# Low halves of stored second-layer weight operands: a subtraction on VectorE or GpSimd, or a negated copy and an accumulating transfer

## The chip, the cores and the metric

The kernel runs on one NeuronCore of a Trainium2 chip. The metric is the device time of one execution in microseconds; the profile comes from one execution taken by the hardware profiler. TensorE multiplies matrices (PE is its matmul row, PEld its weight loads), VectorE is DVE, ScalarE is ACT, GpSimd is POOL, and SyncE, SP, issues transfers here.

## The reference

Attention with two kinds of mask feeds a mixture of four experts without a choice among them: every expert is computed for every token and weighted.

```python
def _attn_ref(q, k, v):                      # (4, 8, 576, 64) float32
    scores = scale * np.matmul(q, k.transpose(0, 1, 3, 2))
    ...                                      # heads 0-3: the last 32 keys; heads 4-7: every 32nd key
    attn = softmax(np.where(masks, scores, -1e9))
    return np.matmul(attn, v)

def _moe_ref(x, domain_probs, w1, w2):       # x (2304, 512), w1 (4, 512, 1024), w2 (4, 1024, 512)
    p = domain_probs / (domain_probs.sum(-1, keepdims=True) + 1e-09)
    for e in range(E):
        h = np.maximum(x @ w1[e], 0.0)
        out += p[:, e:e + 1] * (h @ w2[e])
```

## The kernel before

Every large product is made in three matmul passes: each operand is split into a high half (the value rounded to the type fp32r) and a low half (the value minus its high half), and high x high, low x high and high x low are added in PSUM. An expert's 1024 hidden columns are two units of 512, so there are eight units, 0 to 7.

The tokens are worked in three parts. In the first part, to about 194 us, attention runs and the first 384 tokens go through all units as plain products. The middle part works 896 tokens, unit after unit in the order 7, 0, 1, ..., 6 (the list `first_order`). Its first layer is a Strassen-like scheme of seven products on quarters of the weights and of the inputs (`plan_unit`, products by `product`, line 1082); its second layer is plain (`plan_mm2`, `mm2_t`, line 929). The last part, from about 475 us, works 1024 tokens with the seven-product scheme in both layers and reads its weight operands back from DRAM: `d1` holds the operands of the first layer, `d2` those of the second. The middle part makes them and stores them.

`plan_keep2` is called once for each unit of the middle part. It stores three quarters of the second-layer weights as they are (from the tile `w2t`, whose halves the middle part computes anyway, line 883). The four other operands, s1 to s4, are sums and differences of quarters of `raw2`. Each is built in one of three buffers `tmp` (tokens ws0, ws1, ws2; ws0 is used for s1 and for s4; lines 823 and 826). The function `split` writes its high half by a copy on ACT (line 818) and its low half by a subtraction on DVE or POOL (line 819) into one of the two buffers `wv`, and SP stores that buffer to `d2` (line 894). Operands 0 and 2 use `wv` buffer 0, operands 1 and 3 buffer 1. The same `tmp` buffers are used by `plan_w1` for the first-layer operands of the next unit (tiles s1 to s4, called s in the trace).

In a unit of the middle part the seven products come first (16.8 us) and then the second layer (19 us). ACT copies finished product sums from PSUM into the buffers `u` (line 1284), so that the next product can add into the same bank; it also rounds weights and applies the relu (line 917). DVE joins sums (line 1297), makes low halves of activations (line 920) and accumulates outputs (line 938).

No engine's order is written by hand. The class `Plan` takes operations by `add(engine, duration, function, tokens read, tokens written, priority, ...)` and simulates them at build time with the durations given: at each step the engine and operation that can start first are taken, ties go by priority. An operation of engine "VP" goes to DVE or POOL, whichever would finish it first. An operation with `xfer` is a transfer: to the duration of its issue come 0.7 us, the time given, and 1.4 us until its end. PE's matmuls of the mixture are one fixed list. The result is the order in which each engine's instructions are emitted; at run time each engine works its list in order and waits on semaphores. The dictionary `SHIFT` adds amounts to the priority of single operations, by the operation's number in the order of the `add` calls. Its last entries, 814 to 842, belong to the weights of unit 0, whose operations follow the first call of `plan_keep2` in the numbering.

Of the kernel before, what the change touches and what calls it, by code (L numbers as in the profile page):

```python
# [8 lines left out]
F32 = mybir.dt.float32  # L9
F32R = mybir.dt.float32r  # L10
BF16 = mybir.dt.bfloat16
AF = mybir.ActivationFunctionType
ALU = mybir.AluOpType
# [30 lines left out]
class Plan:  # L44
# [24 lines left out]
    def add(self, eng, dur, fn, reads=(), writes=(), prio=0.0, bank=None, moe=False, cols=0, xfer=None, two=False, lead=None, lag=0.0):  # L69

        o = Op()
        o.eng, o.dur, o.fn, o.prio, o.moe = eng, dur, fn, prio, moe
        o.bank = () if bank is None else bank if isinstance(bank, list) else [bank]
        o.start = None
        o.cols = cols  # L80
        o.xfer = xfer
        o.two = two or eng == "VP"
        o.ready = 0.0
        o.nxt = []
        o.idx = len(self.ops)
        o.prio += SHIFT.get(o.idx, 0.0)
        pre = set()
        for r in reads:
            if r in self.writer:
                pre.add(self.writer[r])  # L90
        for w in writes:
            if w in self.writer:
                pre.add(self.writer[w])
            pre.update(self.readers.get(w, ()))
        pre.discard(o)
        for r in reads:
            self.readers.setdefault(r, []).append(o)
        for w in writes:
            self.writer[w] = o
            self.readers[w] = []  # L100
        o.kind, o.lead, o.early, o.lag = eng, lead, 0.0, lag
        o.wait = o.pre = len(pre)
        for p in pre:
            p.nxt.append(o)
        self.ops.append(o)
# [222 lines left out]
def attn_moe_kernel(  # L328
# [14 lines left out]
    nc = tc.nc  # L343
# [8 lines left out]
    scale = 1.0 / float(D) ** 0.5  # L352
# [77 lines left out]
    add = plan.add  # L430

    def engine(e):
        return nc.vector if e == "DVE" else nc.gpsimd
# [381 lines left out]
    def split(src, tok, hi, lo, name, z):  # L815

        need = [tok, "late1"] if name in ("s1", "s2", "s4") or name[:2] == "wv" else [tok]
        add("ACT", 0.62, lambda: nc.scalar.activation(out=hi(), in_=src(), func=AF.Copy), need, [name + "h"], z)  # L818
        add("VP", VP, lambda e: engine(e).tensor_tensor(  # L819
            out=lo(), in0=src(), in1=hi().bitcast(F32), op=ALU.subtract), need + [name + "h"], [name + "l"], z)  # L820

    def combine(dst, a, b, toks, tok, z):
        add("VP", VP, lambda e: engine(e).tensor_tensor(out=dst(), in0=a(), in1=b(), op=ALU.subtract), toks, [tok], z)

    def total(dst, a, b, toks, tok, z):
        add("VP", VP, lambda e: engine(e).tensor_tensor(out=dst(), in0=a(), in1=b(), op=ALU.add), toks, [tok], z)  # L826
# [24 lines left out]
    def plan_w1(z, step, plain):  # L851

        def t(i):
            return lambda: tmp["s", i]

        if plain:
            plan_quarter(A11, "raw10", "a11", z)
        total(t(0), A21, A22, ["raw10", "raw11"], "ws0", z + step)
        plan_quarter(t(0), "ws0", "s1", z + step)
        combine(t(1), t(0), A11, ["raw10", "ws0"], "ws1", z + 2 * step)  # L860
        plan_quarter(t(1), "ws1", "s2", z + 2 * step)
        if plain:
            plan_quarter(A12, "raw11", "a12", z + 3 * step)
        combine(t(2), A11, A21, ["raw10"], "ws2", z + 4 * step)
        plan_quarter(t(2), "ws2", "s3", z + 4 * step)
        if plain:
            plan_quarter(A22, "raw11", "a22", z + 5 * step)
        combine(t(0), A12, t(1), ["raw11", "ws1"], "ws0", z + 6 * step)
        plan_quarter(t(0), "ws0", "s4", z + 6 * step)
# [9 lines left out]
    def plan_keep2(u, z, step):  # L879


        for n, (nm, i, j) in enumerate((("a11", 0, 0), ("a12", 0, 1), ("a22", 1, 1))):
            add("SP", 0.4, lambda nm=nm, i=i, j=j: nc.sync.dma_start(
                out=d2[u, nm].rearrange("p j h c -> p (j h) c"),
                in_=w2t[:, 2 * j:2 * j + 2, :, 256 * i:256 * i + 256].rearrange("p j h c -> p (j h) c").bitcast(F32)),
                [f"w2{2 * j + a}{h}" for a in range(2) for h in "hl"], [f"d2{u}{nm}"], z + 2 + n, xfer=((1.6, 512),))

        def t(i):
            return lambda: tmp["s", i]

        def keep(n, nm):
            v = n % 2
            split(t((0, 1, 2, 0)[n]), f"ws{(0, 1, 2, 0)[n]}", lambda: late["wv"][v][:, :, 0], lambda: late["wv"][v][:, :, 1], f"wv{v}", z + n * step)
            add("SP", 0.4, lambda: nc.sync.dma_start(out=d2[u, nm], in_=late["wv"][v].bitcast(F32)), [f"wv{v}h", f"wv{v}l"], [f"d2{u}{nm}"],
                z + n * step + 2, xfer=((1.45, 128),))

        total(t(0), B21, B22, ["raw20", "raw21", "late2"], "ws0", z)
        keep(0, "s1")
        combine(t(1), t(0), B11, ["raw20", "raw21", "ws0"], "ws1", z + step)
        keep(1, "s2")  # L900
        combine(t(2), B11, B21, ["raw20", "raw21"], "ws2", z + 2 * step)
        keep(2, "s3")
        combine(t(0), B12, t(1), ["raw20", "raw21", "ws1"], "ws0", z + 3 * step)
        keep(3, "s4")
# [90 lines left out]
    late = {}  # L995
# [369 lines left out]
    for u in range(NU):  # L1365
        z = Z0 + ZU * u
# [6 lines left out]
    z = Z0 + ZU * NU  # L1373
# [128 lines left out]
```

## Time and profile before

| | us |
|---|---|
| Median of 3 runs | 791.96 |
| Lowest and highest run | 791.91, 792.69 |
| Span of the profiled execution | 790.3 |
| Median of the runs over that span | 1.66 |
| PE busy in the span | 780.0 |
| DVE, ACT, POOL busy in the span | 604.0, 325.0, 353.5 |

The span runs from the first to the last instruction of the profiled execution. Busy time of one engine overlaps that of the others. Matmuls are pipelined and their ends are modelled, so a busy PE is not PE at its peak.

### The profile page before, as it was taken

The numbers are of one execution on the slowest core, as the hardware profiler recorded it, in microseconds if no ns is written. First come the engines' busy times: TensorE is split into PE (matmuls) and PEld (weight loads), VectorE is DVE, ScalarE is ACT, GpSimd is POOL, SyncE is SP. The second block draws the span as 40 slices with busy tenths as digits, with TensorE's granted clock in tenths as the row PEclk, the third lists the DMA queues.
The fourth block names the chain that finished last, engine by engine and source line by source line (L and its number), as shares of the span: only waits on it lengthen the run. The fifth ranks groups of instructions, "written<-read, shape, count | busy, mean of one in ns | idle before, by whom it ended". The sixth has DMA issues, their size and how long they took to land.

```text
span 790.3 us, 13805 instructions
## 1 busy us (share of the span) xinstructions
PE 780.0 (99%) x5374; PEld 663.7 (84%) x5377; DVE 604.0 (76%) x828; ACT 325.0 (41%) x597; POOL 353.5 (45%) x265
## 2 busy tenths in 40 slices
PE   7999999999999999999999999999999999999998
PEld 5788888899888889898988888888888888888886
DVE  6988867796888586867768593958787869687886
ACT  4645454653534445263535452524141423232330
POOL 6334223682755152534425170708180817172672
PEclk9999999999999999999999999999999999999999
DMA  9777553157779687775963415837374647555525
GB/s 336 276 272 255 198 180 123 61 199 266 287 276 341 205 302 246 286 262 218 316 217 102 164 40 185 289 140 265 138 268 157 236 162 238 190 183 197 176 80 186
DMA packets 70720, 168.32 MB, mean 213 GB/s; under 512 B 5216, under 2 KB 24320, under 8 KB 70656
## 3 DMA queue, kind: packets, MB, share of 16 engines
q1 hardware_dynamic: 70512, 167.34, 60.4%
q8 instruction: 42, 0.69, 0.3%
q14 instruction: 22, 0.18, 0.1%
q10 hardware_dynamic: 144, 0.11, 0.1%
HBM read 107.64 MB, written 59.79 MB: 212 GB/s over the span
## 4 chain that ended last, share of the span: by engine, by line
PE 97%; DVE 1%; ACT 0%; issue 0%; POOL 0%; DVEq 0%; ACTq 0%
PE mo L1082 23%; PE mo L929 18%; PE ps L1082 18%; PE sc L1082 15%; PE mo L913 9%; PE ps L929 5%; PE sc L929 5%; PE ps L705 2%; PE ps L673 1%; PE sc L561 1%; PE sc L550 1%; PE mo L1408 0%; PE ps L640 0%; DVE wv L819 0%; DVE mx L578 0%
## 5 line engine op out<-in xcount | busy, mean ns | idle before, releaser
L1147 POOL TENSOR_TENSOR q<-q,q 128x512 f32<-128x512 f32 x41 | 60.9, 1492 | 142.4 <-DVE q L1116 141.5
L929 PE MATMUL mo<-w2t,h 128*128 128x512 f32 x336 | 80.8, 389 | 0.0
L929 PEld LDWEIGHTS mo<-w2t,h 128*128 128x128 f32 x336 | 63.1, 188 | 13.0
L929 PE MATMUL mo<-w2t,hs 128*128 128x512 f32 x288 | 70.9, 397 | 0.0
L920 DVE SCALAR_TENSOR_TENSOR h<-c,h 128x448 fp32r<-128x448 f32 x48 | 61.6, 1311 | 2.4 <-ACT h L917 1.0
L929 PEld LDWEIGHTS mo<-w2t,hs 128*128 128x128 f32 x288 | 52.8, 188 | 11.3
L819 POOL TENSOR_TENSOR w2t<-raw,w2t 128x512 fp32r<-128x512 f32 x21 | 31.4, 1503 | 61.4 <-ACT w2t L818 51.3
L819 POOL TENSOR_TENSOR a<-raw,a 128x512 fp32r<-128x512 f32 x17 | 27.7, 1629 | 57.1 <-DVE c L1297 55.4
L1113 DVE TENSOR_TENSOR q<-ps,v 128x512 f32<-128x512 f32 x48 | 33.1, 690 | 25.3 <-PE ps L1082 24.8
L938 DVE SCALAR_TENSOR_TENSOR acc<-mo,pr,acc 128x512 f32<-128x512 f32 x45 | 33.6, 746 | 24.3 <-PE mo L929 24.0
L818 ACT ACTIVATE w2t<-raw 128x512 fp32r<-128x512 f32 x60 | 37.4, 632 | 33.0 <-PE mo L929 18.6
L1208 DVE TENSOR_TENSOR acc<-sc,acc 128x512 f32<-128x512 f32 x57 | 38.5, 685 | 15.7 <-PE sc L1082 15.5
L1104 ACT ACTIVATE v<-mo 128x512 f32<-128x512 f32 x48 | 28.5, 594 | 48.2 <-PE mo L1082 48.2
L913 PE MATMUL mo<-xh,a 128*128 128x384 f32 x192 | 45.5, 340 | 0.0
L1116 DVE SCALAR_TENSOR_TENSOR q<-q,pb 128x512 f32<-128x512 f32 x48 | 42.4, 884 | 1.6
L818 ACT ACTIVATE wv<-tmp 128x512 fp32r<-128x512 f32 x32 | 20.1, 631 | 52.9 <-POOL tmp L826 8.0
L929 PE MATMUL ps<-w2t,h 128*128 128x512 f32 x168 | 40.4, 389 | 0.0
L929 PE MATMUL sc<-w2t,h 128*128 128x512 f32 x168 | 40.4, 389 | 0.0
L1142 ACT ACTIVATE Tb11h<-q 128x512 fp32r<-128x512 f32 x16 | 10.0, 628 | 70.6 <-DVE q L1116 70.6
L1147 DVE TENSOR_TENSOR q<-q,q 128x512 f32<-128x512 f32 x23 | 32.7, 1421 | 6.7 <-POOL Tb21l L1143 6.4
L929 PEld LDWEIGHTS ps<-w2t,h 128*128 128x128 f32 x168 | 31.5, 188 | 6.5
L929 PEld LDWEIGHTS sc<-w2t,h 128*128 128x128 f32 x168 | 31.5, 188 | 6.5
(281 smaller groups left out, 2052.9 us busy)
## 6 DMA issues: line engine op xcount, KB each, us to landing
raw<-in_w SPq DMA_DIRECT2D x28, 1024.0 KB, 6.5
qkS<-in_qk_strided SPq DMA_DIRECT2D x16, 329.0 KB, 7.3
out<-acc SPq DMA_DIRECT2D x17, 256.0 KB, 2.0
vstL<-in_v_local SPq DMA_DIRECT2D x6, 640.0 KB, 5.7
vstS<-in_v_strided SPq DMA_DIRECT2D x8, 384.0 KB, 5.6
qkL<-in_qk_local SPq DMA_DIRECT2D x7, 416.0 KB, 6.2
pb<-dp SPq DMA_DIRECT2D x5, 512.0 KB, 7.6
qkL<-in_qk_local SPq DMA_DIRECT2D x10, 208.0 KB, 5.5
```

The source lines that it names most:

```text
L818: add("ACT", 0.62, lambda: nc.scalar.activation(out=hi(), in_=src(), func=AF.Copy), need, [name + "h"], z)
L819: add("VP", VP, lambda e: engine(e).tensor_tensor(out=lo(), in0=src(), in1=hi().bitcast(F32), op=ALU.subtract), need + [name + "h"], [name ...
L913: nc.tensor.matmul(pt[:, 0:TA], w[:, c % 2, (f % 2) * P:(f % 2) * P + P], (xl if i == 1 else xh)[c], start=j == 0, stop=j == 11)
L920: nc.vector.scalar_tensor_tensor(out=dst(), in0=src(), scalar=0.0, in1=hi().bitcast(F32), op0=ALU.max, op1=ALU.subtract)
L929: nc.tensor.matmul(pt, ht[f][:, ts], wt[f][:, cs], start=j == 0, stop=j == 11)
L938: nc.vector.scalar_tensor_tensor(out=a, in0=pt, scalar=sc, in1=a, op0=ALU.mult, op1=ALU.add)
L1082: nc.tensor.matmul(pt, a[i == 2][:, j, f * P:f * P + P], skewed(b[i == 1][j], TH)[:, cs], start=bool(first) and n == 0, stop=True, skip_gr ...
L1104: add("ACT", TH2 / 1200 + 0.18, lambda: nc.scalar.activation(out=late["u"][i], in_=held[key][:, 0:TH2], func=AF.Copy), [key, "late3"], [f" ...
L1113: add("DVE", DD, lambda: nc.vector.tensor_tensor(out=q(), in0=src(), in1=late["u"][i], op=ALU.add), [key, f"u{i}", "late3"], [tok], min(zz ...
L1116: add("DVE", DD, lambda: nc.vector.scalar_tensor_tensor(out=q(), in0=q() if from_q else src(), scalar=0.0, in1=late["p"][:, c * TH2:c * TH ...
L1147: add("VP", VP, lambda e: engine(e).tensor_tensor(out=dst[0](), in0=a[0](), in1=b[0](), op=ALU.subtract), [a[1], b[1]], [dst[1]], zz - 2.4)
L1208: add("DVE", DD, lambda i=i, key=key: nc.vector.tensor_tensor(out=acc[i], in0=held[key][:, 0:TH2], in1=acc[i], op=ALU.add), [key], tok, zd)
```

## The change

The four operands s1 to s4 of each unit no longer go through `split` but through a new function, `split_moved`. ACT writes the negated, rounded operand into the place of the low half, then the high half as before. A transfer issued from GpSimd's queue then adds the operand itself (fp32, in `tmp`) to the negated high half in place, from SBUF to SBUF: the result is the operand minus its high half, as before. The planner is given 1.0 us on POOL for the issue and 1.5 us for the transfer. It sees one operation more for each operand, so four more for each unit.

```diff
+    def split_moved(src, tok, hi, lo, name, z):
+
+        add("ACT", 0.62, lambda: nc.scalar.activation(out=lo(), in_=src(), func=AF.Copy, scale=-1.0), [tok, "late1"], [name + "l"], z)
+        add("ACT", 0.62, lambda: nc.scalar.activation(out=hi(), in_=src(), func=AF.Copy), [tok, "late1"], [name + "h"], z)
+        add("POOL", 1.0, lambda: nc.gpsimd.dma_start(out=lo().bitcast(F32), in_=src(), accum_op=ALU.add), [tok, name + "l"], [name + "l"], z,
+            xfer=((1.5, 128),))
+
...
         def keep(n, nm):
             v = n % 2
-            split(t((0, 1, 2, 0)[n]), f"ws{(0, 1, 2, 0)[n]}", lambda: late["wv"][v][:, :, 0], lambda: late["wv"][v][:, :, 1], f"wv{v}", z + n * step)
+            split_moved(t((0, 1, 2, 0)[n]), f"ws{(0, 1, 2, 0)[n]}", lambda: late["wv"][v][:, :, 0], lambda: late["wv"][v][:, :, 1], f"wv{v}", z + n * step)
             add("SP", 0.4, lambda: nc.sync.dma_start(out=d2[u, nm], in_=late["wv"][v].bitcast(F32)), [f"wv{v}h", f"wv{v}l"], [f"d2{u}{nm}"],
                 z + n * step + 2, xfer=((1.45, 128),))
```

## Rows read from the trace of the kernel before

**Rows 1.** The page: span, busy times, chain that ended last.

```profile
span 790.3 us, 13805 instructions
...
PE 780.0 (99%) x5374; PEld 663.7 (84%) x5377; DVE 604.0 (76%) x828; ACT 325.0 (41%) x597; POOL 353.5 (45%) x265
...
PE 97%; DVE 1%; ACT 0%; issue 0%; POOL 0%; DVEq 0%; ACTq 0%
```

**Rows 2.** Waits of PE from 190 us to the end: total us, times, longest.

```profile
PE mo L1082 <- ACT u L1284: 0.4, 1, 0.4
```

**Rows 3.** Busy time by stretches: stretch, its length, engines, PE clock, DMA share, GB/s.

```profile
390.00:410.00 20.00, 20.00 (x91) 16.64 (x90) 15.32 (x21) 6.26 (x11) 9.50 (x8) 1.00 0.64 238
...
195.00:446.00 251.00, 250.64 (x1174) 219.81 (x1174) 190.19 (x239) 115.46 (x207) 112.00 (x77) 1.00 0.70 248
```

**Rows 4.** Groups of instructions, 195 to 446 us: the operands' copies and subtractions.

```profile
L818 ACT ACTIVATE wv<-tmp 128x512 fp32r<-128x512 f32 x32 | 20.1, 631 | 52.9 <-POOL tmp L826 8.0 <-POOL tmp L823 6.8 <-DMA d25s<-wv 6.0
...
L819 DVE TENSOR_TENSOR wv<-tmp,wv 128x512 fp32r<-128x512 f32 x24 | 25.6, 1068 | 1.8 <-ACT wv L818 1.8
...
L819 POOL TENSOR_TENSOR wv<-tmp,wv 128x512 fp32r<-128x512 f32 x8 | 11.3, 1412 | 51.2 <-ACT wv L818 51.2
```

**Rows 5.** The tile wv: durations min/median/max ns, and its stores' landing.

```profile
L819 DVE TENSOR_TENSOR wv<-tmp,wv x24: 681/1120/1757, 196.3 to 438.3; 128x512 fp32r<-128x512 f32 x24
L819 POOL TENSOR_TENSOR wv<-tmp,wv x8: 1288/1293/1752, 202.9 to 404.3; 128x512 fp32r<-128x512 f32 x8
...
L894 SPq DMA_DIRECT2D d25s<-wv x4: 320/320/320, 396.9 to 405.6; - x4
...
DMA to landing us min/median/max: 2.6/3.1/5.3
```

**Rows 6.** Transfers by issue: KB each, median us to landing.

```profile
out<-acc SPq DMA_DIRECT2D x17, 256.0 KB, 2.0
```

**Rows 7.** ACT in order of time, 390 to 426 us: start, us, line.

```profile
394.75 0.63 ACT L818 ACTIVATE wv<-tmp 128x512 fp32r<-128x512 f32 x1 [1.34 <-POOL tmp L826]
...
402.36 0.63 ACT L818 ACTIVATE wv<-tmp 128x512 fp32r<-128x512 f32 x1 [5.34 <-DMA d25s<-wv]
...
407.87 2.67 ACT L818 ACTIVATE w2t<-raw 128x512 fp32r<-128x512 f32 x4 [3.64 <-PE ps L929]
411.12 0.55 ACT L1284 ACTIVATE u<-mo 128x448 f32<-128x448 f32 x1 [0.57 <-PE mo L1082]
...
414.32 0.63 ACT L818 ACTIVATE s<-tmp 128x512 fp32r<-128x512 f32 x1 [0.93 <-PE sc L1082]
415.92 0.55 ACT L1284 ACTIVATE u<-mo 128x448 f32<-128x448 f32 x1 [0.97 <-PE mo L1082]
```

**Rows 8.** POOL in order of time, 390 to 426 us.

```profile
394.79 1.56 POOL L823 TENSOR_TENSOR tmp<-tmp,raw 128x512 f32<-128x512 f32 x1
397.05 1.28 POOL L823 TENSOR_TENSOR tmp<-raw,tmp 128x512 f32<-128x512 f32 x1 [0.70 <-DVE wv L819]
```

**Rows 9.** PE in order of time, 408 to 426 us.

```profile
414.52 0.56 PE L1082 MATMUL mo<-t2h,s 128*128 128x448 f32 x2
...
419.32 0.56 PE L1082 MATMUL mo<-t3h,s 128*128 128x448 f32 x2
```

**Rows 10.** The first two units: ACT and PE in order of time.

```profile
195.68 0.62 ACT L818 ACTIVATE wv<-tmp 128x512 fp32r<-128x512 f32 x1
...
205.79 0.52 ACT L1284 ACTIVATE u<-mo 128x448 f32<-128x448 f32 x1
...
206.21 0.54 ACT L1284 ACTIVATE u<-ps 128x448 f32<-128x448 f32 x1
206.36 0.68 PE L1082 MATMUL mo<-t4h,a 128*128 128x448 f32 x2 [0.36 <-ACT u L1284]
...
220.72 0.63 ACT L818 ACTIVATE wv<-tmp 128x512 fp32r<-128x512 f32 x1 [3.41 <-DVE tmp L826]
...
231.75 0.55 ACT L1284 ACTIVATE u<-ps 128x448 f32<-128x448 f32 x1
```

## The prediction

> **What bounds the kernel now.** I read the page first. The span is 790.3 us, the matmul row is busy for 780.0 us of it, and the chain that ended last is 97% PE [rows 1]: before and after the middle part the reader should look for one thing only, what makes PE late. The median of the runs, 791.96 us, lies 1.66 us above the span of the profiled execution. I make the sum on the span and add those 1.66 us.
>
> The waits of PE from 190 us on hold a single entry, 0.4 us on ACT [rows 2]. The table by stretches says the same: from 195 to 446 us, the middle part with its eight units, PE is busy 250.64 of 251.00 us at granted clock 1.00, the 2.4 GHz level, while DVE has 190 us of work, ACT 115 and POOL 112, and the DMA engines are 70% busy [rows 3]. The order of PE's work is a fixed list and none of its matmuls changes. So at most 0.36 us can be won, and the question is whether the longer way of the low halves makes PE wait.
>
> **What is removed.** 32 subtractions (four in each of eight units): 24 on DVE, 1068 ns each, 25.6 us, and 8 on POOL, 1412 ns, 11.3 us [rows 4]. Neither engine was the bound, so they are worth nothing directly; a DVE with 25 us more air is worth nothing either, as PE waited on DVE nowhere [rows 2].
>
> **What is added on ACT.** A second copy for each operand, of the shape of the hi copy, which takes 631 ns [rows 4]: 32 x 0.631 = 20.2 us, and ACT goes from 115 to 136 us in 251 us. The trace shows no copy with a scale; I take it as this row, between the 0.55 us of a 448-column copy and the 0.67 us of a w2t copy [rows 7]. From the second unit on these copies lie in the stretch of second-layer matmuls, where ACT is busy for only 6.26 of 20 us [rows 3]; that idle time hides them. In the first unit nothing does (below).
>
> **What is added on POOL.** 32 transfers, each a 256 KB read, added to 256 KB in place. No transfer of this queue and no accumulating one stands in the trace. How long POOL is held by the issue: from below SP's issue, 0.32 us, from above the longest POOL subtraction, 1.75 us [rows 5]; I take 1.3, an ordinary POOL operation. From the issue's end to the landing: from below 2.0 us, a 256 KB transfer of SP's queue [rows 6], from above 5.3 us, the slowest 512 KB store of the same tile [rows 5]; I take its median, 3.1, since an accumulating 256 KB touches more bytes than a plain one. Call issue to landing T: 2.3 to 7.05, taken as 4.4 us. POOL gets 32 x 1.3 = 42 us and loses 11.3: 143 of 251 us, still idle for four tenths. Behind the waiting transfer stand POOL's own sums and low halves. It waits for ACT's negated copy, 0.63 us, and the flexible operations can go to DVE, which has just lost 25 us. I charge nothing; without that cover it would be at most 0.63 us per transfer on weights that PE needs a phase later. On the DMA engines 8.4 MB are read, added and written in 251 us, at 248 GB/s and 0.70 before [rows 3]; counted as two plain copies that is at most 0.19 more, about 0.89, inside the spread of T.
>
> **What moves: the chain of one unit.** I follow the unit at 390 us (operands of unit 5). Before, the store is issued 2.2 us after the copy starts [rows 5, 7]; now a whole T comes between. The negated copy starts at 394.75 [rows 7], and POOL is in a sum until 396.35 [rows 8]. Issue there, landing at 396.35 + T, store landing 3.1 us later [rows 5]. The second operand's negated copy can start at 396.35, its transfer behind the first about 397.7, its store lands at 400.8 + T. Only then does buffer 1 take the fourth operand: its transfer is issued at about 401.5 + T and lands at 401.5 + 2T, and only then is the first sum buffer free for the next unit's weights.
>
> Who waits for that, in ACT's order: four w2t copies (2.67 us from 407.87), the copies of PSUM into u at 411.12 and 415.92, and the first s copy, at 414.32 [rows 7]. PE writes again into those PSUM banks at 414.52 and 419.32 [rows 9]. The w2t copies may slide until 414.52 - 0.55 - 2.67 = 411.3; the fourth operand's two copies end at 402.1 + T, so T up to 9.2 is hidden. The s copy may slide until 419.32 - 0.55 - 0.63 = 418.1, its sum before it (0.68 us at the shortest on DVE for this shape [rows 5]) must start at 417.4: 401.5 + 2T = 417.4 gives **T = 7.9**. At 4.4 the first sum buffer is free at 410.3, four us before the s copy's old place. So this unit and those like it lose nothing at the value that I take, nor at the top of my bounds, 7.05. Past 7.9 every microsecond of T costs up to two per unit, in the five units 1 to 5; unit 6 has no next unit.
>
> Two units are tighter. In unit 0 the first copy stands 11.03 us ahead of the first u copy (220.72, 231.75), against 16.37 in unit 5 (394.75, 411.12) [rows 7, 10]: 5.3 us less, so its limit is 7.9 - 2.7 = 5.2. Price 0 at 4.4, 3.7 at 7.05; I take 0.3. The first unit works its operands among the products. Its copy starts at 195.68 [rows 10]; with T = 4.4 the first transfer, issued at 196.3, lands at 200.7, the store at 203.8, and the third and fourth operands' four copies (2.5 us) fall between 203.9 and 206.9. There the u copies at 205.79 and 206.21 have no slack: PE waits 0.36 us for them already [rows 10]. Price from -0.36 (that wait disappears) to 3.9 (two copies, 1.26, and a wait of 7.05 - 4.4); I take 0.6.
>
> **The hand-made shifts.** The table SHIFT goes by an operation's number. The first unit gets four more operations, so its eight entries from 814 to 842, which lay on the second unit's weights, now lie on operations four places earlier in the list: a store of the first unit and other splits of the same weights. These weights are made most of a unit ahead of their use. Price 0; to both sides 0.4, the one wait that there is [rows 2].
>
> **The queues passed.** SP's stores of these operands keep their place in the list but start later by about T; the w2t stores and the next load of raw stand behind them. Before, the last of this unit's stores waited already for its low half; the load behind has a full matmul phase until its use. Price 0 up to the limit above. The stores' readers, the ring loads, come after 475 us.
>
> **Sum.** 790.3 + 0.6 + 0.3 + 0 = 791.2 us, and with 1.66 us outside the span **792.9 us**: no measurable change (0.2%, 1.6 us, is what can be told from none here).
>
> **A rule that speaks against it.** The subtractions on DVE take 681 to 1757 ns with a median of 1120 [rows 5]: the same work is stretched when POOL works beside it. The Trainium skill ("SBUF — State Buffer", section "Who interferes with whom") says that DVE in a two-port mode shuts GpSimd out of the port through which it writes the descriptors of its transfers, and infers that two-input operations, which this stretch is full of, do not.
>
> **The rivals.**
> *Collisions in the first two units (0.22).* The way to slower: the extra copies, put ahead of the u copies in ACT's order, wait there for a store that lands late. For it: the 0.36 us wait, at the very place [rows 10]. Against it: the order is rebuilt with the longer times, and the code's own charge for a transfer (1.0 + 0.7 + 1.5 + 1.4 = 4.6 us) is no shorter than my T. It decides from T = 5.2; up to 3.9 + 3.7 = 7.6 us, the middle of it 3: 795 us (793.6 to 799.5).
> *A transfer slower than all my rows (0.10).* With T = 9 units 1 to 5 lose 2 x 1.1 each, 11 us, unit 0 loses 2 x 3.8 = 7.6, the first 1.3 + 4.6 = 5.9: 24.5 us, 816 us. For it: the queue and the kind of transfer are unmeasured. Against: nothing that SP moved at this size took over 5.3 us.
> *Descriptors wait for DVE (0.06).* If POOL could issue only while DVE is idle (15.32 of 20 us busy [rows 3], so 0.23 free), 1.3 us become 5.6 and T = 8.7: by the same terms 8 + 7 + 5.6 = 20.6 us, 813 us. Against it: POOL's sums beside DVE stretch only from 1.28 to 1.56 us [rows 8]. The rule of the Trainium skill quoted above would give this, if it held for two-input operations too.
> *Faster (0.02).* Only by the 0.36 us and by what a new order wins outside PE: 791.6, not measurable; a gain over 0.2% would need matmuls gone.
> The forecast, hidden but for about a microsecond, has 0.60 and its own range 791.6 to 793.5.
>
> **Range and chances.** From 791.6 up into the first rival, 798; above lie the two slow-transfer cases, 0.16, and a little of the first. Faster 0.02, same 0.60, slower 0.38.
>
> **What would show it.** Right: no PE wait over 1 us between 190 and 446 us, 24 + 8 subtractions gone, ACT's 128x512 wv copies 64, ACT's waits for the d2 stores longer but in the second-layer stretches, T near 4.4 between POOL's issue and the d2 store. Wrong: PE waiting for ACT u copies in every unit (T is over 7.9), or for DVE or POOL low halves (POOL is held longer than 1.75 us); a gap in the last 344 us would show that the rebuilt order reaches further than I think.

## The result and the profile after

The changed kernel takes 801.35 us (median of 4 runs, 799.67 to 804.4) against 792.33 us (4 runs, 791.91 to 792.73): ratio 1.0113, 95% interval 1.0096 to 1.013, so 9.0 us slower. The forecast was 792.9 us, its range up to 798.0. The profile below is of the run with 799.67 us, the fastest of the four: it shows 7.6 of the 9.0 us.

The page of the changed kernel (span; busy times; the two large DMA queues with packets, MB and share of 16 engines; the chain that ended last; the group and the landing of the new transfer). Line numbers behind the new function are 7 higher than before.

```profile
span 797.9 us, 13853 instructions
...
PE 782.6 (98%) x5377; PEld 663.9 (83%) x5377; DVE 575.9 (72%) x804; ACT 339.2 (43%) x629; POOL 378.6 (47%) x289
...
q1 hardware_dynamic: 70512, 167.34, 59.2%
q0 software_dynamic: 8704, 8.39, 6.9%
...
PE 93%; DVE 2%; DMA 2%; issue 1%; ACT 1%; POOL 1%; DVEq 0%; ACTq 0%; POOLq 0%
...
L826 POOL DMA_DIRECT2D wv<-tmp x32 | 38.7, 1243 | 54.4 <-ACT wv L824 51.3
...
wv<-tmp POOLq DMA_DIRECT2D x32, 256.0 KB, 6.0
```

The span is 7.6 us longer than before [rows 1], and DMA, which had no share of the chain, has 2% of it. Next the waits of PE from 190 us on, which were one of 0.4 us [rows 2], and the busy times of the middle part.

```profile
PE sc L936 <- DVE h L927: 2.9, 1, 2.9
PE sc L1089 <- ACT u L1291: 2.7, 1, 2.7
PE ps L1089 <- ACT u L1291: 0.9, 1, 0.9
```

```profile
195.00:446.00 251.00, 247.15 (x1156) 216.17 (x1155) 159.09 (x212) 125.95 (x231) 129.88 (x95) 1.00 0.87 271
```

Three waits, 6.5 us, are most of the 7.6. No engine is short of time: DVE has 31 us less than in [rows 3], ACT and POOL gained 10 and 18, and the clock is 1.00. What rose is the DMA share, from 0.70 to 0.87. The waits stand in two places. I compare the starts of the units (the first matmul on b11h): before, every unit lasted 35.87 us; now the unit that starts at 374.30 lasts 40.30, and the unit from 450.48 to the first such matmul of the last part 44.27 where it was 41.35. The others last 35.87 to 36.14, and the first, which contained the wait of [rows 2], has shrunk from 36.52 to 35.87. So the loss is 4.4 and 2.9 us in two units of eight.

The new transfer itself, by its line (issue times in ns; who waited for it, us and times; from issue to landing, us):

```profile
L826 POOL DMA_DIRECT2D wv<-tmp x32: 1168/1200/1396, 197.3 to 453.6; - x32
...
who waited for it (us, times):
  DVE tmp L830: 21.9, 11
  POOL tmp L833: 10.2, 4
  POOL tmp L830: 8.4, 4
  DVE tmp L833: 1.8, 1
...
DMA to landing us min/median/max: 3.8/6.0/11.5
```

Issue to landing is what the prediction calls T. It was taken as 4.4 us and bounded by 7.05. The median is 6.0, the slowest 11.5, and those who wait are the sums that need a `tmp` buffer again. The chain that ended last, in order of time around the first loss (start, us, what):

```profile
377.13 6.92 DMA wv<-tmp
...
384.07 0.69 DVE tmp L830
384.76 0.54 DVE c L1304
...
385.33 0.58 ACT h L924
...
390.33 1.31 POOL tmp L833
...
391.66 1.76 DVE tmp L830
393.42 1.69 DVE h L927 x2
...
397.24 1.19 PE sc L936 x4
```

and three rows of the timeline for the releasers (in brackets the idle time before, and what ended it):

```profile
378.85 1.20 POOL L826 DMA_DIRECT2D wv<-tmp  x1 [0.52 <-ACT wv L824]
...
390.33 1.30 POOL L833 TENSOR_TENSOR tmp<-raw 128x512 f32<-128x512 f32 x1 [2.55 <-DMA wv<-tmp]
...
397.24 1.19 PE L936 MATMUL sc<-w2t,h 128*128 128x512 f32 x4 [2.95 <-DVE h L927]
```

The fourth operand's transfer is issued at 378.85. POOL's first sum for the following first-layer operands may overwrite that buffer only when it has landed, and starts at 390.33, 11.5 us after the issue. DVE's second sum needs the first (391.66), and the low halves of h, which have nothing to do with weights, stand behind that sum in DVE's list. PE waits for them: 2.95 us. A little earlier the third operand's transfer (377.13, 6.92 us) stopped DVE in the same way ahead of c, which made h and then a u copy late: the 0.91 us at 387.38.

A late landing alone does not cost this. In the unit that starts at 414.60 the fourth operand's transfer lands after 10.4 us, and POOL's first sum waits for it too, but PE does not:

```profile
418.57 1.20 POOL L826 DMA_DIRECT2D wv<-tmp  x1 [1.98 <-ACT wv L824]
...
429.09 1.46 POOL L833 TENSOR_TENSOR tmp<-raw 128x512 f32<-128x512 f32 x1 [2.37 <-DMA wv<-tmp]
...
430.63 1.56 POOL L830 TENSOR_TENSOR tmp<-tmp,raw 128x512 f32<-128x512 f32 x1
430.96 0.61 DVE L927 SCALAR_TENSOR_TENSOR h<-mo,h 128x448 fp32r<-128x448 f32 x1
```

Here the planner gave the second sum to POOL, so DVE is free for the low halves of h. The units that start at 302.28 and 338.42 have the same assignment and no listed wait of PE. So the time is lost where a late landing meets an order in which other work stands behind it. This is read from the trace; no run moved that one sum.

The other loss, 2.68 us at 465.33, has the same form with another reader of `tmp`:

```profile
453.63 1.21 POOL L826 DMA_DIRECT2D wv<-tmp  x1 [1.24 <-ACT u L1291]
...
461.30 0.69 DVE L830 TENSOR_TENSOR tmp<-xr 128x512 f32<-128x512 f32 x1 [5.31 <-DMA wv<-tmp]
...
462.63 0.62 DVE L1304 TENSOR_TENSOR c<-ps,u 128x448 f32<-128x448 f32 x1
```

These are among the first sums of activations for the last part (`xr`). They use the same three buffers, and the joins c stand behind them.

Why some transfers land so late is read from the DMA activity of 16 us around those two, 376 to 392 us: queue, packets, MB and share of 16 engines; then transfers, KB each, median us to landing.

```profile
q1 hardware_dynamic: 2570, 4.31, 77.0%
q0 software_dynamic: 544, 0.52, 26.2%
...
raw<-in_w SPq DMA_DIRECT2D x1, 1024.0 KB, 10.1
...
wv<-tmp POOLq DMA_DIRECT2D x2, 256.0 KB, 9.2
```

Together the queues have over 100% of the engines: SP's load of raw, its stores and the two transfers share them. The load, which landed after 8.6 us in the same 16 us of the kernel before, takes 10.1. The engines were nearly full there already in the kernel before (DMA share 0.96):

```profile
376.00:392.00 16.00, 16.00 (x81) 14.85 (x80) 11.35 (x15) 9.56 (x18) 6.34 (x5) 1.00 0.96 327
```

In the changed kernel two transfers, 0.52 MB, take 0.262 x 16 = 4.2 us of all 16 engines; SP's 4.31 MB take 12.3. Per byte the accumulating transfers cost 2.8 times as much here. The transfer issued at 441.90, by contrast, landed 3.8 us later, beside a DMA share of 0.60 (second row, against 1.07 in the first):

```profile
378.90:390.30 11.40, 10.49 (x53) 9.49 (x52) 5.48 (x8) 6.18 (x14) 2.41 (x2) 1.00 1.07 286
...
441.90:445.80 3.90, 3.90 (x19) 3.24 (x18) 1.21 (x2) 1.27 (x3) 2.43 (x2) 1.00 0.60 86
```

### The profile page after: what moved, and what is told of

It is laid out like the page before. It is cut to its first block, busy times and chain, and to the rows that moved or that the text cites. A ratio compares the mean times of both kernels' runs of the same rounds, so it can differ in the third digit from the quotient of the medians.

```text
span 797.9 us, 13853 instructions
## 1 busy us (share of the span) xinstructions
PE 782.6 (98%) x5377; PEld 663.9 (83%) x5377; DVE 575.9 (72%) x804; ACT 339.2 (43%) x629; POOL 378.6 (47%) x289
## 4 chain that ended last, share of the span: by engine, by line
PE 93%; DVE 2%; DMA 2%; issue 1%; ACT 1%; POOL 1%; DVEq 0%; ACTq 0%; POOLq 0%
PE mo L1089 21%; PE mo L936 18%; PE ps L1089 16%; PE sc L1089 15%; PE mo L920 8%; PE ps L936 5%; PE sc L936 5%; PE ps L705 2%; DMA wv<-tmp 2%; PE sc L561 1%; PE ps L673 1%; PE sc L550 1%; PE mo L1415 1%; DVE tmp L830 0%; DVE h L927 0%
## 5 line engine op out<-in xcount | busy, mean ns | idle before, releaser
L826 POOL DMA_DIRECT2D wv<-tmp x32 | 38.7, 1243 | 54.4 <-ACT wv L824 51.3
L819 POOL TENSOR_TENSOR w2t<-raw,w2t 128x512 fp32r<-128x512 f32 x20 | 29.2, 1468 | 60.6 <-ACT w2t L818 50.5
L927 DVE SCALAR_TENSOR_TENSOR h<-c,h 128x448 fp32r<-128x448 f32 x48 | 52.7, 1119 | 2.3 <-ACT h L924 1.2
L936 PE MATMUL ps<-w2t,h 128*128 128x512 f32 x168 | 40.4, 389 | 0.0
L818 ACT ACTIVATE s<-tmp 128x512 fp32r<-128x512 f32 x32 | 20.2, 631 | 42.6 <-POOL tmp L830 11.6
```

Source lines behind the costliest of these rows:

```text
L819: add("VP", VP, lambda e: engine(e).tensor_tensor(out=lo(), in0=src(), in1=hi().bitcast(F32), op=ALU.subtract), need + [name + "h"], [name ...
L826: add("POOL", 1.0, lambda: nc.gpsimd.dma_start(out=lo().bitcast(F32), in_=src(), accum_op=ALU.add), [tok, name + "l"], [name + "l"], z, xf ...
L927: nc.vector.scalar_tensor_tensor(out=dst(), in0=src(), scalar=0.0, in1=hi().bitcast(F32), op0=ALU.max, op1=ALU.subtract)
L936: nc.tensor.matmul(pt, ht[f][:, ts], wt[f][:, cs], start=j == 0, stop=j == 11)
```

## The experiments

The theory to be tested (the landing theory): the transfers land late, because they are dear and the DMA engines are full just then, and what is held in order behind a late landing costs the time. Against it stand: the rebuilt order and the added copies; the added traffic and issues, whoever waits; and a transfer that is slow by its kind or its queue whatever runs beside it. All times are medians; the kernel before ran beside them at 792.31 us (first four) or 792.87 us (the rest).

| experiment | us | ratio to before (95%) | PE's waits, us | landing min/median/max, us |
|---|---|---|---|---|
| addition on GpSimd | 793.12 | 1.0009 (0.9999 to 1.0018) | 0.6 | none |
| first three operands | 794.31 | 1.0025 (1.0015 to 1.0035) | 1.7 | 3.7/5.6/8.5 |
| longer times in the plan | 805.86 | 1.018 (1.0163 to 1.0197) | 9.8 | 3.8/6.5/10.3 |
| a fourth sum buffer | 800.81 | 1.0104 (1.0089 to 1.0119) | 6.1 | 3.8/7.5/11.8 |
| only the fourth operand | 792.2 | 0.9992 (0.9983 to 1.0001) | none | 3.7/3.8/5.6 |
| light loads | 796.08 | 1.0038 (1.0023 to 1.0053) | 3.5 | 3.8/4.6/10.4 |
| light loads, kernel before | 792.5 | 0.9997 (0.9988 to 1.0007) | 0.4 | none |
| shadow transfer | 797.39 | 1.0054 (1.0037 to 1.007) | 0.6 | 4.0/6.7/12.0 |
| shadow at the end | 793.48 | 1.0007 (0.9997 to 1.0016) | 0.6 | 4.0/6.7/11.6 |
| pad, kernel before | 796.73 | 1.0052 (1.0034 to 1.0069) | 0.4 | none |
| quarter of the bytes | 794.96 | 1.0022 (1.0013 to 1.0032) | 1.8 | 2.5/4.9/8.3 |
| plain transfer | 794.51 | 1.0019 (1.001 to 1.0029) | 1.5 | 2.5/4.8/8.3 |

**The same order without the transfer.** An addition on GpSimd takes the transfer's place; every engine's order is that of the changed kernel.

```diff
-        add("POOL", 1.0, lambda: nc.gpsimd.dma_start(out=lo().bitcast(F32), in_=src(), accum_op=ALU.add), ...
+        add("POOL", 1.0, lambda: nc.gpsimd.tensor_tensor(out=lo(), in0=src(), in1=lo().bitcast(F32), op=ALU.add), ...
```

> Everything as after the change, in the same order on every engine, but in the place of the accumulating transfer GpSimd itself adds the operand to the negated high half (a 128x512 addition of 1.3 to 1.7 us). Theory A (the transfer lands 6.0 us after its issue, up to 11.5, where the plan counts 4.6, and holds its two buffers as long; in-order engines stand behind): the stalls go, 791.5 to 793.5 us. Rival B (the new order, the 32 more ACT copies and the load on GpSimd are the cost, whatever the transfer takes): stays at 799 us or more. Rival C (the transfers' bytes slow the loads and stores of the other queue): also 792 us, so this run alone does not part A from C.

793.12 us: with 64 copies on ACT, 32 operations of 1.3 us on POOL and the rebuilt order 0.8 us are lost, which the interval hardly tells from nothing; the trace has 0.6 of them in a wait for h at 393.56. So about 8.2 of the 9 us belong to the transfer.

**Three operands, then only the fourth.**

```diff
-            split_moved(t((0, 1, 2, 0)[n]), ...
+            (split_moved if n in (0, 1, 2) else split)(t((0, 1, 2, 0)[n]), ...
```

> Only operands one to three of each unit go by copy and transfer, the fourth by the subtraction as before. Theory A by way of the fourth operand's late landing: 792.5 to 795 us. Rival C, in proportion to bytes: three quarters of 9 us, 799 us. Rival B, in proportion to copies: 799 us.

794.31 us. The other way round, `n in (3,)`:

> Only the fourth operand of each unit goes by the copy and the transfer, the first three by copy and subtraction. The three others alone cost 2.0 us (794.3). If the fourth operand's late landing, which holds the first sum buffer for the next unit, is where most of the 9 us arise (theory A as now put): 797 to 800, and PE's waits are again on u copies and on h low halves behind a sum that waits for that transfer. If the loss needs all four transfers in a chain (two buffers, each held for a whole landing twice): 792.5 to 795, and the fourth lands at 5 to 7 us.

792.2 us, no wait of PE at all. I had expected a good part of the loss here, since the late landing at 378.85 is the fourth operand's. Alone it is issued at 368.00 in that unit, in the second-layer stretch (as six of its eight transfers are), and the median lands in 3.8 us. So 2.0 us for three and nothing for one do not add up to 9. Each of these runs has an order of its own. With all four the third and the fourth transfer stand among the products of the next unit in the units from 230.40 to 414.60, beside SP's load of raw. The late landings did not push them there: in the first experiment, with no transfer, the fourth operand's addition stands at 378.46 as well. It is the planner's order, made with its times for four transfers.

**Planner told of longer transfers** (issue 1.2 us, and 3.0 us more until the end) **and a sum buffer of its own for the fourth operand.**

```diff
                 o.end, free[e] = transfer(s, dur, o.xfer)
+                if e == "POOL":
+                    o.end += 3.0
```

> The change as it is, but the planner counts 1.2 us for the issue and 3 us more until the landing (about 8 us in all, between the median of 6.0 and the 11 us of the fourth operand). Theory A, with the mismatch between plan and chip as the way it costs: other work is put ahead of what waits, 792.5 to 796 us. If the latency is too long for any order with these buffers: 797 to 802 us, as without. Rival C: 799 us or more.

805.86 us, worse than without, and covered only by the "799 us or more" of the traffic rival: the plan spreads the work, its last transfer is issued at 478.2 instead of 453.6, and PE waits above all for low halves of weights (5.2 of 9.8 us).

```diff
-            split_moved(t((0, 1, 2, 0)[n]), f"ws{(0, 1, 2, 0)[n]}", ...
+            split_moved(t(n), f"ws{n}", ...
...
-        combine(t(0), B12, t(1), ["raw20", "raw21", "ws1"], "ws0", z + 3 * step)
+        combine(t(3), B12, t(1), ["raw20", "raw21", "ws1"], "ws3", z + 3 * step)
```

> The change as it is, but the fourth operand has a sum buffer of its own, so its transfer (10 to 11 us in most units) no longer holds the buffer in which the next unit's first sum is made. Theory A by way of the shared sum buffer: 792.5 to 796 us. If the cost goes by the store buffers wv or by traffic (rival C): 799 us or more.

800.81 us, in the band of the other two causes, the store buffers and the traffic. The trace shows that most of the stall moved into the first unit, which lasts 41.74 us instead of 35.87, and that a sum waits for a landing there too:

```profile
197.51 2.67 POOL L826 DMA_DIRECT2D wv<-tmp  x2 [13.79 <-ACT wv L824]
...
206.37 0.69 DVE L833 TENSOR_TENSOR tmp<-raw 128x512 f32<-128x512 f32 x1 [5.95 <-DMA wv<-tmp]
207.15 0.63 ACT L818 ACTIVATE s<-tmp 128x512 fp32r<-128x512 f32 x1 [4.48 <-DVE tmp L833]
...
210.88 0.67 PE L1089 MATMUL mo<-t4h,a 128*128 128x448 f32 x2 [3.98 <-ACT u L1291]
```

The transfer of 197.51 is awaited until 206.37; an s copy waits for the sum in ACT's order, and behind it the u copy that PE needs. More `wv` buffers were not tried: a third takes 4 KB per partition, and 3.75 KB are free.

**Light loads.** The loads of raw in the middle part move a quarter of their bytes, in the changed kernel and in the kernel before.

```diff
+        if "wv" in late and ks == slice(0, NKD):
+            ks = slice(0, 1)
         nc.sync.dma_start(out=raws[which][:, ks], in_=src.rearrange("(k p) f -> p k f", p=P)[:, ks])
```

> This kernel is the changed one, but the loads of raw weights in the middle part move only a quarter of their bytes (the first of four slices; the other three quarters are left out, so the weights of later units are wrong there). Orders and instructions stay the same. Theory A (the accumulating transfers are slow because SP's loads and stores use the same DMA engines at that time): the median issue to landing falls from 6.0 to about 4 us, the fourth operand's from 10 to 11 us to under 6, PE's waits from 190 us on (6.5 us before) fall under 1 us, and the time is 793 to 795. Theory B (the transfer is slow by itself, by its kind or its queue): landing stays at 6.0 in the median and near 11 at the slowest, and the time stays at 800 to 802.

> The control for the light loads: the kernel before with the same quarter loads (three quarters of each raw load of the middle part left out). PE was its bound and waited for no load, so both theories expect no change: 791.5 to 792.5 us. If it is faster or slower than that, the difference has to be taken off what the light loads do to the changed kernel.

796.08 us against 792.5: with the same instructions and the same order 3.6 us are left of 9.0. The median landing falls to 4.6 us, the slowest only to 10.4, and PE still waits 3.5 us (all three were expected lower, and the time at 793 to 795). So the traffic beside the transfers is a large part of the cause, but their own and the stores' share stays.

**The same transfers, but nobody waits.** To the addition on GpSimd comes an accumulating transfer of 224 KB per operand, from activations in SBUF into two buffers that nobody reads.

```diff
+        def moved():
+            nc.gpsimd.tensor_tensor(out=lo(), in0=src(), in1=lo().bitcast(F32), op=ALU.add)
...
+            nc.gpsimd.dma_start(out=late["shadow"][late["n"] % 2][:, :, 0:224], in_=xr["r2"][0][:, 0:448]..., accum_op=ALU.add)
...
         late["wv"] = [p.tile([P, 2, 2, 256], F32R, name=f"wv{i}") for i in range(2)]
+        late["shadow"] = [p.tile([P, 2, 232], F32, name=f"shadow{i}") for i in range(2)]
```

> GpSimd computes the low half by an addition (as in the first experiment, 793.1 us), and beside it issues an accumulating transfer of 224 KB per operand into two buffers of its own that nobody reads. So the queue, the issue and nearly all of the traffic are there, and only the waiting for the landing is gone. Theory A (the cost is what waits for the late landing): within 1.5 us of the first experiment, 792.5 to 794.5. Rival C (the cost is the added traffic or the issues on POOL, which slow SP's loads and stores and POOL's sums, whoever waits for the transfer itself): 797 to 802.

797.39 us, in the band of the traffic rival. But PE's listed waits are 0.6 us, and every unit of the middle part lasts 36.3 us or more, where 35.87 was the rule. The loss is even over all units, which no wait explains; the new buffers had moved h, u and c by 3712 bytes. So the same with the buffers allocated last, and the kernel before with nothing but a pad of 3712 bytes at that place:

> The shadow experiment again with its two extra buffers allocated behind all others of the stretch, so that the addresses of h, u and c are those of the changed kernel. In the first shadow run (797.4 us) the units lasted 36.3 to 36.4 us instead of 35.87, although PE's listed waits were 0.6 us: the second-layer matmuls themselves came at a longer distance, which could be the moved addresses of h (3712 bytes further) and not the traffic. Theory A with the addresses as the cause of that: 792.8 to 794.5 us, units of 35.87. Rival C (traffic or POOL's issues): again 796.5 to 798, units of 36.3.

> The kernel before with a pad of 3712 bytes per partition ahead of h, u and c, nothing else. If the addresses of h make the second-layer matmuls slower, its units last 36.3 us too and the time is 795 to 796.5; if not, 791.5 to 793.

793.48 and 796.73 us. The pad alone costs 3.9 us; the shadow transfers, which land as late as those of the changed kernel (4.0/6.7/11.6), cost nothing over the addition on GpSimd alone (ratio 1.0007 against 1.0009). With seven eighths of the bytes, the traffic and the issues hardly count by themselves; what costs the 8 us is what waits for the landing. The pad's even loss is in the second-layer matmuls, here from 240 to 425 us in the kernel before and then in the pad kernel (busy us, mean ns):

```profile
L929 PE MATMUL mo<-w2t,h 128*128 128x512 f32 x204 | 49.1, 389 | 0.0
L929 PE MATMUL mo<-w2t,h 128*128 128x512 f32 x204 | 50.3, 395 | 0.0
```

**Fewer bytes, and no addition.** The transfer over 32 of 128 partitions, and the transfer of all as a plain copy:

```diff
-nc.gpsimd.dma_start(out=lo().bitcast(F32), in_=src(), accum_op=ALU.add)
+nc.gpsimd.dma_start(out=lo()[0:32].bitcast(F32), in_=src()[0:32], accum_op=ALU.add)
...
+nc.gpsimd.dma_start(out=lo().bitcast(F32), in_=src())
```

> The changed kernel with each accumulating transfer over 32 of the 128 partitions (64 KB instead of 256; the low halves of the other 96 partitions stay the negated high halves, so a part of the weights is wrong). Kind, queue, issue, order and waits stay. Theory A (what counts is when the transfer lands): landing 2 to 3.5 us, no PE wait over 1 us, 792.3 to 794. Rival (the wait on a transfer of GpSimd's queue costs by its kind, by fixed latency or by its issue): 798 to 802.

> The changed kernel with the same 256 KB transfer on the same queue, but a plain copy without the addition (the low halves are then the whole operands, wrong weights). If the addition makes the transfer long: landing 3 to 4.5 us in the median and 792.5 to 795 us. If it is the queue or the traffic beside it: landing near 6.0 and 798 to 802 us as before.

794.96 and 794.51 us: both give back over 6 of the 9 us. Not all fell where I expected: the quarter's median landing, 4.9 us, is longer (2 to 3.5) and its time above 794, and the plain copy's landing, 4.8 us, lies above 3 to 4.5. So a quarter of the bytes is late too, 2.5 us at the shortest and 8.3 at the longest. The plain copy shows what the addition costs; its queue on the page, and the place of the first loss in its timeline:

```profile
q0 software_dynamic: 2560, 8.39, 3.0%
```

```profile
379.16 0.72 POOL L826 DMA_DIRECT2D wv<-tmp  x1 [1.00 <-ACT wv L824]
...
387.51 1.30 POOL L833 TENSOR_TENSOR tmp<-raw 128x512 f32<-128x512 f32 x1 [0.79 <-DMA wv<-tmp]
...
394.48 1.20 PE L936 MATMUL sc<-w2t,h 128*128 128x512 f32 x4 [1.06 <-DVE h L927]
```

The same bytes go in 80 packets per transfer instead of 272 and take 3.0% of the engines instead of 6.9%. And at one place, in one order, there are now three sizes of the same wait, with the addition on GpSimd as the one without a transfer:

```profile
378.46 1.29 POOL L826 TENSOR_TENSOR wv<-tmp,wv 128x512 fp32r<-128x512 f32 x1 [0.43 <-ACT wv L824]
...
386.21 1.68 POOL L833 TENSOR_TENSOR tmp<-raw 128x512 f32<-128x512 f32 x1
...
393.56 1.21 PE L936 MATMUL sc<-w2t,h 128*128 128x512 f32 x4 [0.62 <-DVE h L927]
```

From the fourth operand's place to the first sum 7.75, 8.35 and 11.48 us pass; PE's wait behind it is 0.62, 1.06 and 2.95. My estimate from the first of these: in this order a landing of up to 7.75 us would be hidden by what stands ahead of the sum in POOL's list. Past it the wait grows, by 2.3 us for 3.7. With the 0.91 us that the third operand costs ahead of it, the unit from its first product to the next one's lasts 36.83, 37.24 and 40.30 us, so 3.5 us more for 3.7.

## Why the prediction was wrong

**The failed step is the term T.** I took 4.4 us from the bounds 2.3 and 7.05, both made of SP's transfers [rows 5, 6], and from it the price 0 for steady units, also "at the top of my bounds, 7.05". Measured: 3.8 in a quiet stretch, 6.0 in the median, 11.5 beside SP's load and stores. One value for all transfers was the mistake: the median lies inside the bounds, the two transfers ahead of the large waits, 11.4 us at 378.85 and 7.6 us at 453.63, lie outside. Two things were missing, and the runs change each by itself: the addition (without it 4.8 in the median, 8.3 at the slowest, 794.51 us) and the hour of the transfer (with light loads 796.08 us). The bounds came from transfers that were not dear, and from a mean DMA share: 0.70 to "about 0.89" was right (0.87), but I put it "inside the spread of T" and did not look for the stretches in which the engines were already full. [rows 3] had 0.64 in the one that I drew; the 16 us into which the third and fourth transfers went had 0.96. A smaller slip went the other way: the views give the landing from the start of the issue, so I counted SP's issue, 0.32 us, twice and had T and its bounds that much too high.

**The limit was nearly right, the unit was not.** I had T = 7.9 as the point from which a steady unit loses; the place that decided shows 7.75. That is partly luck: I drew the unit of before, with the fourth transfer 32 us after the unit's first product (405.9 - 373.84), and in the rebuilt order it is issued 40.4 us after it (378.85 - 338.42), among the products of the next unit, beside SP's load of raw. The reader that suffered was also another: not the s copy ahead of a u copy, but DVE's sum ahead of the low halves of h. My price past the limit, two for one in five units, was far too high; 801 us is not the 816 of the rival with T = 9, since two of eight units lost. Other units had late landings too (10.4 and 10.8 us at 418.57 and 342.39) and lost nothing (35.88 us each); there the planner had put the second sum on POOL. I left that choice of the rebuilt order out.

**A reader was left out.** That "unit 6 has no next unit" is wrong: the last part's first sums of activations use the same `tmp` buffers. They waited 5.31 us, and PE 2.68. This is the second step that failed: the stretch from the last unit's first product to the last part's lost 2.9 us, which I had at nothing.

**What held.** PE as the bound, and no gain to be had: the best variant, only the fourth operand, is not to be told from before. The negated copy costs 626 ns (taken 631), the issue on POOL 1.20 us (taken 1.3), and copies, order and an addition in place of each issue 0.8 us in the run without transfers (taken 0.9 as the price of the first two units). That these two agree is luck, as the place was wrong: the first unit lost nothing, its 0.36 us even disappeared, and the rival of collisions in the first two units fell; it came up only with the fourth sum buffer. The shifted entries seem to cost nothing: in the first experiment, which displaces them in the same way, the unit whose weights they move lasts 35.88 us. No run with corrected entries was made.

**The rival of the descriptors** fell: POOL's issue takes 1168 to 1396 ns throughout. The shortest is one beside a DVE that is busy all the time with operations of two inputs; the issue of 377.13, with DVE idle, takes 1.20 us.

```profile
338.62 0.75 DVE L945 SCALAR_TENSOR_TENSOR acc<-sc,pr,acc 128x512 f32<-128x512 f32 x1 [0.68 <-PE sc L936]
...
339.24 1.17 POOL L826 DMA_DIRECT2D wv<-tmp  x1
339.33 1.29 DVE L819 TENSOR_TENSOR w2t<-raw,w2t 128x512 fp32r<-128x512 f32 x2
```

The Trainium skill ("SBUF — State Buffer", section "Who interferes with whom") infers that `tensor_tensor` of DVE, with its two inputs, leaves GpSimd's descriptor writing alone. This trace agrees: 1168 ns beside it, 1200 without.

## What to carry to other kernels

A transfer put in the place of an engine's operation is priced by its landing beside all the traffic of its moment, not by quiet transfers of the same size: find the stretches in which the DMA share is near 1 and bound from those. Then list every reader and writer of each buffer that it holds, the next stage's too, and ask what stands behind them in each engine's order: here one unit lost over 4 us, and others with landings nearly as late nothing. An engine with idle time is no cover for a buffer that is held.

## What was unexpected of the hardware

An accumulating transfer from SBUF to SBUF went in 272 packets for 256 KB where the plain copy went in 80, took 1.7 us of all 16 engines (6.9% of 797.9 us over 32) against 0.74 (3.0% of 792.9 us), and its issue held POOL for 1.20 us against 0.72. With a quarter of the bytes the median landing was 4.9 us instead of 6.0.

Moving h, u and c by 3712 bytes made each 512-column second-layer matmul 395 ns in the mean instead of 389, each unit from the second to the seventh 36.3 to 36.4 us instead of 35.87, and the kernel 0.52% slower, with no wait to show for it. Which of the addresses does it was not tried.
